# RWKV-7 attention and a GELU MLP on one core: the weights' last conversion step as an integer addition on GpSimd, a scheduler with a refitted picture of the chip, and a search over priorities in the opening

## The chip, the cores and the metric

The kernel runs on one core of a Trainium2 chip. The metric is the device time of one execution in microseconds (us), smaller is better. Before the change the median of three executions is 723.49 us (722.95 to 725.37). The execution that the profiler recorded took 728.5 us, of which 726.7 us lie between its first and last instruction (the span).

## The reference, cut to what matters

For 4 batches, 8 heads, 768 time steps and a head size of 40, a state matrix is carried from step to step; its readings form 3072 tokens of 320 numbers, which go through an MLP with 2048 hidden units:

```python
for t in range(S):
    y[:, :, t] = np.einsum('bhd,bhde->bhe', rt, state)
    Sa = np.einsum('bhde,bhe->bhd', state, at)
    state_decay = state * wt[:, :, None, :] - np.einsum('bhd,bhe->bhde', Sa, bt)
    state = state_decay + np.einsum('bhd,bhe->bhde', vt, kt)
x = y.transpose(0, 2, 1, 3).reshape(B * S, H * D)
h = x @ w_in
g = h * (1.0 / (1.0 + np.exp(-1.702 * h)))
return g @ w_out
```

The inputs are float32, except `w_in` and `w_out`, which come as float64. The kernel receives these as 64-bit words and makes float32 of them on the chip.

## The kernel before, in words

**Tiling.** The 768 steps are cut into 12 chunks of 64 steps. One chunk of two batches is a unit, so there are 24 units, and units 2c and 2c+1 together are chunk c. Inside a unit the recurrence becomes a triangular system. `logarithm` and `decay` make the cumulated decay factors FT, GT and G by running sums (`ps_cum`, `ps_cumc`) and exponentials on ScalarE (ACT). `prep` multiplies them into the inputs (`ak`, `b`, `kh`, `bh`) and makes score matrices (`ps_A`, `ps_RV`). `inverse` inverts the triangular matrix in five levels of doubling (`ps_N`, `ps_level`, `ps_Q`, `ps_T`); each level is a TensorE (PE) product, a copy out of PSUM by ACT or VectorE (DVE), and a DVE transposition. The first four units use a variant of fewer, wider steps (`plain_level`). `solve` puts the state of two units before in (`ps_zT`, `ps_rz`, `ps_B`), solves (`ps_X`, then M, L861), and reads out (`ps_y`, L867 to L900). The result x (L907) goes to DRAM and comes back transposed as `xT` (L917, L921), once for each unit. Only then can `mlp(c)` start: 160 `up` products for a chunk (`ps_up`), the GELU on ACT (`g`, L942), and for each half of a chunk 64 `down` products (`ps_down`), then an addition and a store (L966 to L968). In float32 each product of the program shows as two matmul and two weight-load instructions in the trace.

**The weights.** `weight` (L406 to L447) brings in eight pieces of 128x1280 weights, four of `w_in` (0 to 3), four of `w_out` (4 to 7). Each is 1280 KB of float64 in HBM. The raw words land in one of a few places (`extra`, parts of `w_sb`, or the not yet used part of `xT_all`). The steps are: `rebased` on ACT (L422) scales the high word, read as a float32; `bounded` on DVE (L426) clamps it; `exponent`, two DVE instructions (L430, L431), shifts it left by 3 and keeps sign and exponent apart; `fraction` on DVE (L434) multiplies the low word by 2^-52 and by that power of two; `joined` on DVE (L438) adds both as float32. Pieces 5, 6 and 7 are loaded into a place that an earlier piece must have left first.

**What sets the order.** There is no order in the program text. Every step is a task with a rank, the engines that could do it with a cost in ns for each, what it reads and writes, and a PSUM buffer pair. `Plan.order` is a list scheduler: it runs a picture of the chip forward and gives each free engine the able task of the lowest rank. The picture has a cost for DMA transfers (LATENCY, RATE, SPREAD), the blocks of 256 instructions that PE must fetch (BLOCK, FETCH, and BESIDE for a fetch beside a DMA transfer)[...]. `paced` repeats that four times to spread the MLP products evenly. The tasks are then issued in the order found; each engine, and SP's DMA queue, works through its list strictly in order. ACT needs one table for Ln and Exp and another for GELU. Before, the exponentials of units 4 on are preceded by a load of the table at L542, whether it is the active one or not, and their cost in the picture has 1300 ns for it.

Of the kernel before, what the change touches and what calls it, by code (L numbers as in the profile page):

```python
# [50 lines left out]
class Task:  # L51
    def __init__(self, rank, engines, fn, pair, most, size):
        self.instr, self.sbuf = engines.pop("instr", 0), engines.pop("sbuf", False)
        self.rank, self.fn, self.pair, self.most, self.size = rank, fn, pair, most, size
        self.engines = engines
        self.after, self.then, self.release = set(), [], 0.0


class Plan:
# [5 lines left out]
    BLOCK, FETCH, BESIDE, AHEAD = 256, 3550.0, 0.4, 300.0  # L65
    DELAY = {"PE": 300.0, "DVE": 60.0, "ACT": 60.0, "POOL": 150.0, "SP": 800.0}

    BEGIN = {"PE": 0.0, "ACT": 3300.0, "DVE": 4100.0, "POOL": 9500.0, "SP": 800.0}
    LATENCY, RATE, SPREAD = 1200.0, 400.0, 1.3
# [5 lines left out]
    def add(self, rank, engines, fn, reads=(), uses=(), writes=(), room=(), pair=None, most=None, size=0):  # L75

        t = Task(rank, engines, fn, pair, most, size)
        for key in uses:  # L80
            self.used.setdefault(key, []).append(t)
        for key in reads:
            t.after.update(self.made[key])
            self.used.setdefault(key, []).append(t)
        for name, n in (*writes, *room):
            if name in self.slots:
                old = (name, n - self.slots[name])
                t.after.update(self.made.get(old, ()), self.used.get(old, ()))
        for key in writes:
            self.made.setdefault(key, []).append(t)  # L90
        if pair is not None:
            writers = self.of_pair.setdefault(pair, [])
            t.after.update(o for o in writers if "PE" in o.engines)
            writers.append(t)
        t.after.discard(t)
        self.tasks.append(t)

    def order(self):
# [11 lines left out]
        running, last = [], {}  # L110

        def fits(t):
            if t.pair is None or t.pair in held:
                return True
            clear = sum(p <= now for p in pairs)
            if t.most is None:

                return clear > len({o.pair[0] for o in able if o.most is not None and o.pair not in held and not any(k[0] == o.pair[0] for k in many)})
            return clear > 0 and sum(k[0] == t.pair[0] for k in many) < t.most
# [3 lines left out]
        def fetch(at):  # L123
            took = self.FETCH
            for _ in range(3):
                beside = sum(max(0.0, min(y, at + took) - max(x, at)) for x, y in running[-8:])
                took = self.FETCH + self.BESIDE / self.SPREAD * beside
            return took
# [4 lines left out]

        def fetched(t, start):

            at, left, ns, block = start, t.instr, t.engines["PE"] / t.instr, begun
# [8 lines left out]
        def ahead(t):  # L145

            return (issued % self.BLOCK + t.instr) * fetch(begun) / self.BLOCK - (now + t.engines["PE"] - begun)

        while coming or able:
# [4 lines left out]
            for e in free:  # L154
                if free[e] <= now:
                    took = next((t for t in able if e in t.engines and fits(t) and unread(t, e) <= now), None)
# [5 lines left out]
            if not took:  # L162
                later = [x for x in (*free.values(), *pairs, *(unread(t, e) for t in able for e in t.engines)) if now < x < float("inf")]
                now = min(later + ([coming[0][0]] if coming else []))
                continue
# [3 lines left out]
            end = now + t.engines[e]  # L169
            if e == "PE":  # L170
                end, begun = fetched(t, now)
                issued += t.instr
# [5 lines left out]
            if e == "SP":  # L178
                wire = max(wire, end + self.LATENCY)
                running.append((wire, wire + self.SPREAD * t.size / self.RATE))  # L180
# [21 lines left out]
        assert len(out) == len(self.tasks)  # L202
# [20 lines left out]


@with_exitstack
def rwkv7_gelu_quick(ctx: ExitStack, tc: tile.TileContext, time_d, v_d, w_d, wc_d, ak_d, b_d, rv_d, w_in, w_out, out):
# [16 lines left out]
    ROUNDS, WINDOW, SHARE = 4, 5000.0, 1.0  # L243
    RANKS = [14, 16, 20, 24, 35, 37, 39, 41]
# [74 lines left out]
    padded(nc.vector, rv_t[0])  # L319

# [18 lines left out]
    starts = single("starts", [128, 8, 33])  # L339
    nc.gpsimd.memset(starts, 1.0)  # L340
    nc.gpsimd.memset(starts[:, :, 0], 0.0)
# [15 lines left out]
    for t in ak_t[1], b_t[1], rv_t[1]:  # L357
        padded(nc.gpsimd, t)
# [47 lines left out]
    def weight(n, rank, src):  # L406
# [21 lines left out]
        def exponent(t):  # L428

            nc.vector.tensor_scalar(word(INT32, 1), scale(), 3, -2 ** 23, ALU.logical_shift_left, ALU.bitwise_and)  # L430
            nc.vector.tensor_single_scalar(scale(), scale(), 3, op=ALU.logical_shift_left)  # L431

        def fraction(t):
            nc.vector.scalar_tensor_tensor(word(FP32, 1), in0=word(UINT32, 0), scalar=2.0 ** -52, in1=word(FP32, 1),  # L434
                                           op0=ALU.mult, op1=ALU.mult)

        def joined(t):
            nc.vector.tensor_add(scale().bitcast(FP32), scale().bitcast(FP32), word(FP32, 1))  # L438

        one, two = 170.0 + 0.48 * PIECE, 150.0 + 1.05 * PIECE  # L440
# [4 lines left out]
        plan.add(rank, {"DVE": 2 * one, "sbuf": True}, exponent, reads=T("bounded"), writes=T("exponent"))  # L445
        plan.add(rank, {"DVE": two, "sbuf": True}, fraction, reads=T("exponent"), writes=T("fraction"))
        plan.add(rank, {"DVE": two, "sbuf": True}, joined, reads=T("fraction"), writes=T("weight"))  # L447
# [18 lines left out]

    def load(i):
        for name, of, src, n in (("ak", ak_of, ak_d, 1024), ("time", time_of, time_d, 2 * DM), ("b", b_of, b_d, 512),
                                 ("rv", rv_of, rv_d, 1024), ("RV", RV_of, v_d, 320)):
            rows = [slice(p.start, p.start + D) for p in HALF] if name in ("ak", "b", "rv") else [slice(0, 128)]  # L470

            def go(t, name=name, of=of, src=src, rows=rows):
                for p in rows:
# [3 lines left out]
                     size=sum(p.stop - p.start for p in rows) * n * 4)  # L477
# [10 lines left out]

    def logarithm(i):
        def go(t):  # L490
            if i >= BY_PE:
                nc.scalar.activation(wc_of(i), wc_of(i), ACT.Ln)
            nc.scalar.activation(logw_of(i), logw_of(i), ACT.Ln)
        plan.add(10 * i - 30, {"ACT": (1080.0 if i >= BY_PE else 450.0) + (1300.0 if i >= EARLY + 2 else 0.0)}, go,
# [10 lines left out]
    def decay(i):  # L505
# [19 lines left out]
        def exp_of_product(t):  # L525
            sums = psum(t, "")[:, :, :260].rearrange("p b (j t) -> p b j t", t=65)
# [13 lines left out]
        def exp_channel(t):  # L540
            if i >= EARLY:
                nc.scalar.preload_act_table_set("natural_log_exp_and_others")  # L542
# [8 lines left out]
        if i < BY_PE:  # L551
            plan.add(R, {"ACT": 2400.0}, exp_of_product, reads=T("cum"), writes=T("FT", "GT", "wch"), pair=("cumc", i))
        else:
            plan.add(R, {"ACT": 1600.0 + (1300.0 if i >= EARLY else 0.0)}, exp_channel, reads=T("cum", "sums"), uses=T("wc"),
                     writes=T("FT", "GT", "wch"))
        plan.add(R, {"ACT": 460.0}, lambda t: nc.scalar.activation(G_of(i), psum(t, "")[:, :, :160], ACT.Exp, scale=-1.0),
# [69 lines left out]
    def inverse(i):  # L626
# [36 lines left out]
        def turned(rank, source, reads, n, dst, writes):  # L663
# [10 lines left out]
            plan.add(rank, {"POOL": 1390.0, "DVE": 700.0, "ACT": 1000.0, "sbuf": True}, spread, reads=[key("ES", n, 6)], writes=writes)  # L674
# [254 lines left out]
    def mlp(c):  # L929
# [11 lines left out]
        def gelu(q):  # L941
            plan.add(-45, act(1024), lambda t: nc.scalar.activation(  # L942
# [61 lines left out]
    tasks = plan.paced(list(paces.values()), ROUNDS, WINDOW, SHARE)  # L1004
# [83 lines left out]
```

## Time and profile before

| what | value |
|---|---|
| median of three executions | 723.49 us |
| the profiled execution / its span | 728.5 us / 726.7 us |
| mean granted PE clock | 0.978 |
| PE busy | 677.6 us (93%) |
| DVE / ACT / POOL busy | 430.0 / 356.8 / 187.9 us |
| PE busy, 0 to 150 us | 113.1 us |
| PE busy, 150 to 600 us | 443.0 us |
| first `ps_up` / first `ps_down` matmul starts at | 78.4 / 99.7 us |
| last matmul starts at | 721.5 us |

A page has the busy time of each engine, the span in 40 slices (busy share in tenths; PEclk is the clock that TensorE was granted, in tenths of full speed), and groups of instructions by line, engine, operation and tiles (out<-in), with count, busy time, mean duration, and what ended the idle time before them. The chain of waits is followed back from the last instruction to what released it. The table by stretches gives each engine's busy time in a stretch of the span, then the granted clock and the share of time in which the DMA engines were busy. "issue" stands for a wait that no semaphore explains.

### The profile page before, as it was taken

How to read it: one execution, taken by the hardware profiler on the slowest of the kernel's cores; microseconds unless marked ns; L12 is line 12 of the kernel's file. 1: busy time of each engine (PE TensorE's matmuls, PEld its weight loads, DVE VectorE, ACT ScalarE, POOL GpSimd, SP SyncE). 2: the span in 40 equal slices, each digit the busy share in tenths (PEclk: the TensorE clock that was granted, in tenths of full speed). 3: DMA queues.
4: the chain of work that ended last, by engine and by line, in shares of the span. 5: the costliest groups of instructions: out<-in, count | busy, mean ns of one | idle time of the engine just before them, and what ended most of it. 6: DMA issues, size and time to landing. Idle time of an engine off the chain costs nothing.

```text
span 726.7 us, 43527 instructions
## 1 busy us (share of the span) xinstructions
PE 677.6 (93%) x20256; PEld 572.5 (79%) x20256; DVE 430.0 (59%) x739; ACT 356.8 (49%) x705; POOL 187.9 (26%) x260
## 2 busy tenths in 40 slices
PE   4566997999999999999999999999999989999997
PEld 4555885799788789888888878887889978897564
DVE  6578888956667666666756655755666556431000
ACT  4455655557554554545465455457446446342120
POOL 8104143432431331330350320431530310200000
PEclk9879998999999999999999999999999999999999
DMA  7963542332251341351450440441340230110000
GB/s 216 351 251 93 165 124 86 107 96 78 91 145 55 109 120 49 88 158 32 119 136 22 116 130 31 119 118 39 120 112 23 85 95 5 40 49 30 18 5 20
DMA packets 31861, 69.82 MB, mean 96 GB/s; under 512 B 5056, under 2 KB 14272, under 8 KB 30656
## 3 DMA queue, kind: packets, MB, share of 16 engines
q1 hardware_dynamic: 31680, 67.03, 30.5%
q8 instruction: 159, 2.61, 1.4%
q14 instruction: 22, 0.18, 0.1%
HBM read 59.15 MB, written 7.86 MB: 92 GB/s over the span
## 4 chain that ended last, share of the span: by engine, by line
PE 83%; DVE 5%; issue 3%; ACT 3%; DMA 3%; POOL 2%; SPq 1%; POOLq 0%; DVEq 0%; ACTq 0%
PE ps_down L275 28%; PE ps_up L275 26%; PE ps_level L275 8%; PE ps_y L275 5%; PE ps_B L275 4%; PE ps_X L275 2%; DMA ak<-in_ak 2%; PE ps_Q L275 2%; PE ps_N L275 1%; PE ps_T L275 1%; PE ps_rz L275 1%; PE ps_A L275 1%; PE ps_RV L275 1%; PE ps_zT L275 1%; PE ps_cum L275 1%
## 5 line engine op out<-in xcount | busy, mean ns | idle before, releaser
L275 PE MATMUL ps_up<-xT_all,w_sb 64*64 64x256 f32 x3840 | 249.1, 378 | 2.6 <-ACT g L942 1.5
L275 PE MATMUL ps_down<-w_sb,g 64*64 64x320 f32 x3072 | 244.4, 434 | 3.1 <-DVE w_sb L438 2.5
L275 PEld LDWEIGHTS ps_up<-xT_all,w_sb 64*64 64x64 f32 x3840 | 160.6, 133 | 26.7 <-ACT g L942 1.8
L275 PEld LDWEIGHTS ps_down<-w_sb,g 64*64 64x64 f32 x3072 | 136.2, 134 | 45.3 <-issue 3.1
L670 ACT ACTIVATE EX<-ES,quads 128x256 f32<-128x256 f32 x116 | 52.6, 501 | 49.7 <-DVE ES L665 49.3
L591 POOL TENSOR_TENSOR kh<-time,G 128x320 f32<-128x320 f32 x24 | 22.0, 918 | 185.3 <-PE ps_y L275 91.4
L942 ACT ACTIVATE g<-ps_up 128x1024 f32<-128x1024 f32 x48 | 49.1, 1023 | 40.4 <-PE ps_up L275 40.1
L275 PEld LDWEIGHTS ps_level<-W,EX 64*64 64x64 f32 x2560 | 57.3, 134 | 7.4 <-ACT EX L670 1.4
L716 DVE TENSOR_TENSOR E<-two,ps_level 128x256 f32<-128x256 f32 x80 | 33.2, 415 | 40.3 <-ACT W L714 39.8
L275 PE MATMUL ps_level<-W,EX 64*64 64x64 f32 (+1 forms) x2560 | 55.7, 218 | 0.7 <-ACT EX L670 0.3
L714 ACT COPY W<-ps_level 128x512 f32<-128x512 f32 x51 | 29.8, 585 | 44.0 <-PE ps_level L275 43.9
L275 PE MATMUL ps_level<-PT,EX 64*64 64x64 f32 (+2 forms) x1280 | 36.6, 251 | 11.4 <-DVE EX L686 7.2
L968 DVE TENSOR_TENSOR ob<-ob,ps_down 128x320 f32<-128x320 f32 x24 | 11.6, 484 | 59.4 <-ACT ob L966 59.1
L275 PEld LDWEIGHTS ps_level<-PT,EX 64*64 64x64 f32 x1280 | 34.3, 152 | 15.2 <-DVE EX L686 7.0
L907 POOL TENSOR_TENSOR x<-zr,FT 128x128 f32<-128x128 f32 x84 | 42.8, 539 | 10.4 <-ACT zr L899 10.2
L583 POOL TENSOR_TENSOR ak<-ak,FT 128x512 f32<-128x512 f32 x21 | 27.3, 1299 | 53.2 <-DMA ak<-in_ak 26.2
L845 ACT COPY B<-ps_B 128x416 f32<-128x416 f32 x36 | 18.2, 506 | 44.1 <-PE ps_B L275 43.6
L275 PE MATMUL ps_y<-RV,kh 64*64 64x104 f32 x768 | 36.4, 252 | 2.3 <-DVE M L861 2.2
L665 DVE STREAM_TRANSPOSE ES<-E 128x256 f32<-128x256 f32 x80 | 35.6, 445 | 3.9
L275 PE MATMUL ps_y<-M,bh 64*64 64x104 f32 x768 | 36.5, 252 | 1.3 <-issue 1.3
L275 PEld LDWEIGHTS ps_y<-RV,kh 64*64 64x64 f32 x768 | 30.1, 134 | 6.4 <-DVE M L861 2.4
L861 DVE TENSOR_TENSOR M<-ps_X,later 128x832 f32<-128x832 f32 x24 | 24.5, 1021 | 17.6 <-PE ps_X L275 17.6
(140 smaller groups left out, 1132.9 us busy)
## 6 DMA issues: line engine op xcount, KB each, us to landing
ak<-in_ak SPq DMA_DIRECT2D x48, 160.0 KB
time<-in_time SPq DMA_DIRECT2D x24, 320.0 KB
rv<-in_rv SPq DMA_DIRECT2D x48, 160.0 KB
xT_all<-x_dram SPq DMA_DIRECT2D x48, 160.0 KB
wc<-in_wc SPq DMA_DIRECT2D x20, 264.0 KB
logw<-in_w SPq DMA_DIRECT2D x24, 160.0 KB
b<-in_b SPq DMA_DIRECT2D x48, 80.0 KB
RV<-in_v SPq DMA_DIRECT2D x24, 160.0 KB
```

The source lines that it names most:

```text
L275: nc.tensor.matmul(o, lhsT, rhs, start=start, stop=True, skip_group_check=True)
L583: plan.add(R, {"DVE": 690.0, "POOL": 1270.0, "sbuf": True}, lambda t: of(t.engine).tensor_mul(ahT(), ahT(), FT_of(i)), reads=T("ak", "FT") ...
L591: plan.add(R + 4, {"POOL": 870.0, "DVE": 490.0, "sbuf": True}, lambda t, n=n, dst=dst: of(t.engine).tensor_mul(dst(i)[:, :, :D], by_head(t ...
L665: plan.add(rank, dve(256), lambda t: nc.vector.transpose(ES(n), source(t)), writes=[key("ES", n, 6)], **reads)
L670: nc.scalar.activation(dst[:, :, h], ES(n), ACT.Copy, scale=quads[:, h, :1])
L714: plan.add(rank, any2(512), lambda t: copy(t.engine)(tiles_of(W(n + 1)), blocks(psum(t, ""), 64)), writes=[key("W", n + 1, 5)], pair=pair)
L716: plan.add(rank, dve(256), lambda t: nc.vector.tensor_sub(tiles_of(E(n + 1)), every(two32, [128, 2, 4, 32]), blocks(psum(t, ""), 64)[:, :, ...
L845: plan.add(R, any2(416), lambda t: copy(t.engine)(dst(), psum(t, "")[:, :, :208]), writes=[("Bv", i)] if x and c > 0 else T("B"), pair=(na ...
L861: plan.add(R + 1, dve(832), lambda t: nc.vector.tensor_tensor(M_of(i).rearrange("p (j b) n -> p b j n", b=2), psum(t, "")[:, :, :416].rear ...
L907: of(t.engine).tensor_mul(x[:, b ^ u, b], both(i)[:, at, :64], FT_of(i)[:, at])
L942: plan.add(-45, act(1024), lambda t: nc.scalar.activation(g_of(c * NQ + q).rearrange("p m r n -> p r m n"), psum(t, "").rearrange("p r (m ...
L968: plan.add(-45, dve(320), lambda t: nc.vector.tensor_add(ob_of(serial), ob_of(serial), psum(t, "")[:, 1, :DM]), reads=[("ob", serial)], wr ...
```

## The change

**Weights.** The last steps of a piece are different. `shifted` (one DVE instruction) shifts the scaled high word left by 3 and keeps everything; `rounded` (one DVE instruction) multiplies the low word by 2^-29 and rounds it to an integer in place; `joined` adds both words as 32-bit integers on GpSimd. The DVE instructions of a piece go from five to three, and POOL gets one of 128x1280.

**The picture.** DMA latency, rate and start times, ACT costs, and the cost of a fetch beside a transfer have new values, transfers over 1 MB with one of their own. Matmuls count double when PE was busy for less than 45% of the last 2.6 us. ACT's active table is followed: Ln, Exp and GELU tasks carry its name, a switch costs 1290 ns, and the table of Ln and Exp is loaded only where the order has a switch to it.

**The search.** After `paced`, `refined` tries 300 times to move the ranks of some tasks that start in the first 140 us of the picture by random amounts, and keeps a move if the picture ends earlier.

**The opening by hand.** The zero fills of `b` and `rv` for the second unit go from POOL to DVE, that of `ak` ahead on POOL, `starts` later. The loads of a unit go ak, b, rv, RV, time instead of ak, time, b, rv, RV, and the first two units' have earliest times (CLEAR).

```diff
-        def exponent(t):
-            nc.vector.tensor_scalar(word(INT32, 1), scale(), 3, -2 ** 23, ALU.logical_shift_left, ALU.bitwise_and)
+        def shifted(t):
             nc.vector.tensor_single_scalar(scale(), scale(), 3, op=ALU.logical_shift_left)
-        def fraction(t):
-            nc.vector.scalar_tensor_tensor(word(FP32, 1), in0=word(UINT32, 0), scalar=2.0 ** -52, in1=word(FP32, 1),
-                                           op0=ALU.mult, op1=ALU.mult)
+        def rounded(t):
+            nc.vector.tensor_single_scalar(word(INT32, 1), word(UINT32, 0), 2.0 ** -29, op=ALU.mult)
         def joined(t):
-            nc.vector.tensor_add(scale().bitcast(FP32), scale().bitcast(FP32), word(FP32, 1))
+            nc.gpsimd.tensor_tensor(out=scale(), in0=scale(), in1=word(INT32, 1), op=ALU.add)
...
-        plan.add(rank, {"DVE": 2 * one, "sbuf": True}, exponent, reads=T("bounded"), writes=T("exponent"))
-        plan.add(rank, {"DVE": two, "sbuf": True}, fraction, reads=T("exponent"), writes=T("fraction"))
-        plan.add(rank, {"DVE": two, "sbuf": True}, joined, reads=T("fraction"), writes=T("weight"))
+        plan.add(rank, {"DVE": one, "sbuf": True}, shifted, reads=T("bounded"), writes=T("parts"))
+        plan.add(rank, {"DVE": one, "sbuf": True}, rounded, reads=T("rebased"), writes=T("parts"))
+        plan.add(rank, {"POOL": add}, joined, reads=T("parts"), writes=T("weight"))
...
-    BLOCK, FETCH, BESIDE, AHEAD = 256, 3550.0, 0.4, 300.0
+    OPENING = 140000.0
+    BLOCK, FETCH, AHEAD = 256, 3528.0, 300.0
+    BESIDE, LARGE, BESIDE_LARGE = 0.35, 1e6, 0.63
+    COLD, WINDOW, SHARE = 2.0, 2600.0, 0.45
+    SWITCH = 1290.0
...
-    LATENCY, RATE, SPREAD = 1200.0, 400.0, 1.3
+    LATENCY, RATE, SPREAD = 2010.0, 417.0, 1.3
...
+            if e == "ACT" and t.table:
+                t.load, table = t.table != table, t.table
+                end += self.SWITCH if t.load else 0.0
...
+    def refined(self, tries, seed):
...
+        groups = {}
+        for t in self.tasks:
+            if abs(t.rank) < 10000 and t.start < self.OPENING:
+                groups.setdefault((t.fn.__code__.co_firstlineno, t.rank), []).append(t)
+        keys, rng, best = list(groups), random.Random(seed), end()
+        for _ in range(tries):
+            some = rng.sample(keys, max(1, int(len(keys) * rng.choice((0.003, 0.01, 0.03, 0.1)))))
+            width = rng.choice((0.6, 2.0, 5.0))
...
+            new = end()
+            if new < best:
+                best = new
+            else:
+                for t, rank in old:
+                    t.rank = rank
...
         def exp_channel(t):
-            if i >= EARLY:
-                nc.scalar.preload_act_table_set("natural_log_exp_and_others")
+            tables(t)
...
-    tasks = plan.paced(list(paces.values()), ROUNDS, WINDOW, SHARE)
+    plan.paced(list(paces.values()), ROUNDS, WINDOW, SHARE)
+    tasks = plan.refined(TRIES, SEED)
```

## The prediction

> **What bounds the kernel now.** I read the slices of the page first, then the table by stretches, the waits of TensorE (PE), and the chain of waits. The slices show two different kernels in one:
>
> ```profile
> PE   4566997999999999999999999999999989999997
> PEclk9879998999999999999999999999999999999999
> DMA  7963542332251341351450440441340230110000
> ```
>
> From the eighth slice on (127 us) PE is busy throughout; nothing that another engine does there can gain much. The opening is where time is lost. The stretches (us of PE, PEld, DVE, ACT, POOL, then clock, DMA share, GB/s):
>
> ```profile
> 0.00:20.00 20.00, 10.13 (x346) 8.82 (x347) 13.44 (x21) 8.42 (x27) 15.35 (x51) 1.00 0.76 234
> 20.00:50.00 30.00, 18.34 (x509) 16.28 (x509) 19.47 (x26) 15.48 (x32) 1.48 (x2) 0.72 0.95 335
> 50.00:78.40 28.40, 19.58 (x769) 18.20 (x768) 24.08 (x29) 14.50 (x33) 9.55 (x11) 0.88 0.29 87
> 78.40:110.00 31.60, 30.97 (x844) 26.98 (x840) 26.53 (x33) 19.60 (x32) 9.49 (x9) 1.00 0.51 158
> 110.00:135.00 25.00, 19.06 (x629) 14.55 (x625) 21.62 (x30) 13.06 (x30) 5.99 (x6) 0.86 0.22 75
> 135.00:727.00 592.00, 579.52 (x17192) 487.63 (x17184) 324.89 (x603) 285.70 (x554) 146.07 (x182) 1.00 0.27 77
> ```
>
> The reader is to see two weak places: up to 78.4 us (the first `ps_up` matmul) PE is half idle and slow, and at 110 to 135 us there is a second hole while DVE is the busiest engine. Who is waited for in the first 130 us (us in total, times, longest):
>
> ```profile
> PE ps_level L275 <- DVE EX L686: 7.2, 5, 2.3
> PE ps_level L275 <- issue: 3.8, 2, 2.8
> PE ps_A L275 <- issue: 3.4, 1, 3.4
> PE ps_down L275 <- DVE w_sb L438: 2.0, 1, 2.0
> ```
>
> "issue" is PE waiting for its own instructions. The trace's instruction queue moves 16 KB packets for PE; they start at 24.04, 31.64, 38.70 and 45.79 us, 7.1 to 7.6 us apart while the DMA engines are 95% busy, but 3.6 to 4.6 us apart from 58.96 to 79.3 us. The hole at 110 us is named by the chain (start, us, what):
>
> ```profile
> 108.92 1.28 ACT L542
> ...
> 113.33 2.33 DVE extra L434
> ...
> 117.50 1.75 DVE w_sb L438
> ...
> 119.30 4.54 PE ps_down L275 x32
> ```
>
> The `down` products wait for the last pieces of weights, which wait for DVE: the hole is conversion work in DVE's queue. The 32 matmuls after it take 4.54 us, against 2.15 for 32 at 99.93 in the same chain.
>
> **A sum for the whole span.** At full pace the chain has 80 `ps_up` in 4.32 us (54.0 ns), 224 `ps_down` in 15.07 (67.3 ns) and 64 `ps_y` in 1.43 (22.3 ns); 32 matmuls of 64 columns or fewer follow each other in 0.46 (14.4 ns), and the 96, 128 and 160 columns lie on the same line. Over all 20,256 that is 647.2 us: 207.4 for up, 206.8 for down, 233.0 for the rest. I call time minus the PE work ahead of a point its loss:
>
> - first `ps_up`: 78.4 - 30.7 = 47.7
> - first `ps_down`: 99.7 - 50.4 = 49.3 (so 1.6 more)
> - `ps_y` of unit 3 (133.45 in the chain): 133.4 - 73.6 = 59.8 (10.5 more)
> - end of the last matmul: 722.0 - 647.2 = 74.8 (15.0 more, evenly over the chunks)
>
> 647.2 + 74.8 + 4.7 (last addition and store) is the span of 726.7; with 1.8 around it 728.5. The median of the runs is 5.0 below that one execution, so I take differences from the sum and apply them to 723.5.
>
> [...] L426 takes 784 ns at best and 1889 at 70.36 us, where POOL's multiplications L583 and L588 run. [...]
>
> **The change part by part.**
>
> *DVE's share of the weights.* Undisturbed durations: 0.80 (L426), 0.83 (L430), 0.83 (L431), 1.50 (L434), 1.46 (L438), so 5.42 us for a piece, 43.4 for eight. After: 0.80 + 0.83 + `rounded`. This reads every second word and writes in place; 0.83 is the price of L430, which writes that way, 1.50 that of L434, which reads that way with a second tensor. I take 0.83: 2.46 for a piece, 19.7 for eight, 23.7 less. The high end costs 5.4 of that. The built order gives DVE other work back (two zero fills, copies of Tc). Counted through with such durations, the work ahead of M of unit 3 (L861) falls from 100.4 to 84.5 us, and that up to the last weight step from 99.4 to 77.3.
>
> *POOL's additions.* The nearest rows:
>
> ```profile
> L583 POOL TENSOR_TENSOR ak<-ak,FT 128x512 f32<-128x512 f32 x21 | 27.3, 1299 | 53.2 <-DMA ak<-in_ak 26.2 <-ACT FT L545 18.5 <-PE ps_level L275 3.9
> L591 POOL TENSOR_TENSOR kh<-time,G 128x320 f32<-128x320 f32 x24 | 22.0, 918 | 185.3 <-PE ps_y L275 91.4 <-issue 72.2 <-ACT EX L670 15.1
> ```
>
> From 918 to 1299 ns for 192 more elements is 1.98 ns each: 1299 + 768 x 1.98 = 2.8 us. [...] Eight are 22.6 us[...]. POOL was busy 20 of the 80 us from 30 to 110, so it fits. Behind the additions are queued: T of unit 0 behind piece 0's, `ak` of unit 2 behind piece 1's, x of unit 0 behind piece 2's, x of unit 1 behind piece 3's; `ps_Q`, then `xT` and the first `ps_up`, wait for them. I take nothing for it, because each piece's last DVE step lies beside the PE and DVE steps that these wait for anyway; without that cover 2.8 us each. For the lock I take 5 us of longer DVE instructions in all (0.6 an addition), low 0, high 12.
>
> *Loads.* In the built SP order pieces 0 to 4 come before `ak`, `b` and `rv` of unit 2, so 11.2 MB instead of 8.4 lie up to `ak` of unit 2: 2.8 MB at 335 GB/s, 8.4 us later, about 43 instead of 35. Its first products now stand behind 468 others instead of 368, at about 50 us, so that hides it; without that, up to 8.
>
> *Order up to the first up.* There 868 products now stand ahead, not 812, with 32.9 us of PE work. A block of 256 instructions is 64 products, so 56 more cost 0.9 block of 3.9 us: 81.9, a loss of 49. Against this, one interval in the series of packets (50.04 to 58.96) is 8.9 us with PE waiting for ACT and DVE; the new picture prices cold PE and fetches beside large transfers, so I take it down to 4.0: first up at 77.0, loss 44.
>
> *The hole.* Before, M of unit 3 ended at 131.2, 30.8 after its DVE work. With the same 30.8 and the lock's 5 it ends at 84.5 + 35.8 = 120.3, and `ps_y` starts 2.2 later as it did before (131.2 to 133.4), at 122.5. Its PE work is 74.0: loss 48.5. I add 1.5 for pieces 6 and 7: they should be ready at about 104 and 110 and are due at about 111 and 114. So 50 instead of 59.8.
>
> *Tables and the rest.* Table loads go from 38 to 34 of 1283 ns, 5 us of ACT, off the path after 135. Loss there stays 15, within 3.
>
> Sum: 44 + 2 + 4 + 15 = 65 instead of 74.8, 9.8 less: span 716.9, execution 718.7, and 723.5 - 9.8 = 713.7 us for the median.
>
> **The rivals.**
>
> - *Supply bound (0.20).* Instruction fetch paces the opening, so reordering gains nothing there (loss 49), and the hole keeps 6: 49 + 2 + 6 + 15 = 72, 720.7 us. For it: 7 us packets and the "issue" waits. Against: five waits on DVE in `ps_level`.
> - *All fits (0.13).* First up at 73 (loss 40), no hole (0.5), 13 later: 55.5, 704.2 us.
> - *GpSimd in the way (0.10), slower.* Three of the four results queued behind additions come 2.8 us late, and these are on the serial path: loss 49 + 8.4 at the first up, then 2 + 4 + 15: 78.4, 727.1 us. It decides from a first `ps_up` after about 86.7 us (32.9 + 53.8). For it: POOL works strictly in order[...]. Against: POOL's long idle stretches (185.3 us before L591).
> - *Moved, not removed (0.07).* The picture's end is earlier, the chip's is not: later chunks lose what the opening gains, 723.5 us.
>
> **How the numbers follow.** My case has 0.50 and gives 713.7. A measurement tells about 0.3%, 2.2 us, from no change. Faster: 0.50 + 0.13 + 0.13 of the first rival = 0.76; same 0.07 of it + 0.05 = 0.12; slower 0.10 + 0.02 = 0.12. The range, 705 to 722, leaves out half of the best case below and most of the two last above.
>
> **What would show it.** Five DVE groups for weights become three with 0.8 us means; a POOL group of 128x1280 at 2.8 us; M of unit 3 near 120; no `ps_down` wait over 1 us on weights; `ps_up` from 75 to 79 us. I am wrong if `ps_up` starts after 82, if the hole stays, or if loss after 135 us grows by more than 3.

## The result and the profile after

The changed kernel takes 713.75 us (median of 4 runs, 707.54 to 715.64) against 723.22 us before (median of 4, 720.94 to 725.37). The ratio is 0.986, with a 95% interval of 0.983 to 0.990: some 10 us less. The profiled execution of the changed kernel took 715.64 us with a span of 713.9, the longest of its four; the one of before took 728.5 with 726.7. So the two profiles lie 12.8 us apart, and some 3 us of that are the choice of executions.

Line numbers in the changed file are higher: the matmuls are L330 (L275 before), the weight steps L482 (bounded), L486 (shifted), L490 (rounded) and L494 (added on GpSimd), the table loads L549 (16 of them, for exponentials) and L1008 (17, for gelu), 1283 ns each.

The slices of the page of after, to be held against those of before:

```profile
PE   4667899999999999999999999999999999999997
PEclk9879999999999999999999999999999999999999
DMA  7955351431441341341432241251341230111000
```

PE stays at nine from the sixth slice on instead of from the eighth, and the span ends 13 us sooner. The same stretches (us of PE, PEld, DVE, ACT, POOL, then clock, DMA share, GB/s):

```profile
20.00:50.00 30.00, 19.67 (x578) 18.07 (x573) 21.02 (x30) 15.62 (x26) 12.20 (x8) 0.73 0.86 316
50.00:78.40 28.40, 20.79 (x837) 18.41 (x832) 23.68 (x30) 17.38 (x43) 17.82 (x17) 0.93 0.56 174
78.40:110.00 31.60, 29.74 (x872) 27.66 (x876) 25.72 (x42) 16.53 (x28) 12.43 (x6) 1.00 0.35 108
110.00:135.00 25.00, 25.00 (x817) 22.91 (x813) 20.89 (x35) 15.74 (x32) 12.16 (x10) 1.00 0.38 111
135.00:714.00 579.00, 568.40 (x16880) 466.56 (x16872) 318.01 (x593) 273.55 (x528) 137.21 (x174) 1.00 0.26 76
```

The second hole is gone: PE is busy for all of the 25 us from 110 to 135, at full clock, where it had 19.06 at 0.86. The first weak place remains almost as it was: 19.7 of 30 us and a clock of 0.73 from 20 to 50. GpSimd went from 1.5 to 12.2 us busy there. Who is waited for in the first 130 us:

```profile
PE ps_level L330 <- issue: 5.5, 3, 2.4
PE ps_N L330 <- DMA ak<-in_ak: 5.2, 1, 5.2
PE ps_X L330 <- DVE T L853: 3.3, 2, 2.9
PE ps_cumc L330 <- issue: 2.1, 1, 2.1
```

The 7.2 us for the spread P (`EX`) are down to 0.9, and there is no wait of `ps_down` for weights; "issue" now leads. (The 5.2 us for `ak` lie at the very start, up to 10.6 us; there the kernel before waits 3.9 us for `rv`.)

What "issue" stands for can be read from the 16 KB packets of instructions. In each of the two profiles, 159 of them come for 20,256 matmuls and as many weight loads: 255 of these a packet, near the 256 that the prediction counts for a block. In both profiles each such wait of more than 0.8 us in the first 135 us ends 1.2 to 1.6 us after one of these packets has landed: before, PE goes on at 22.89 us after a packet that landed at 21.38, and at 29.94 after 28.60; after the change at 23.13 after 21.84, and at 29.80 after 28.52. So I read these as waits for instructions. The packet times that the prediction gives stand 11.2 us too late on the clock of the span: its first four packets start at 12.83, 20.43, 27.50 and 34.59 us, and its interval of 8.9 us runs from 38.84 to 47.76.

The chain of waits at the place of the old hole (start, us, what):

```profile
117.65 1.01 PE ps_down L330 x13
118.66 0.68 PE ps_X L330 x30
...
121.61 1.11 PE ps_down L330 x14
122.71 1.39 PE ps_y L330 x62
```

It is matmuls alone, in the lines left out too: DVE is no longer on it. The groups of the weight steps:

```profile
L486 DVE TENSOR_SCALAR w_sb<-w_sb 128x1280 int32<-128x1280 int32 x8 | 11.9, 1487 | 0.1
L482 DVE TENSOR_SCALAR w_sb<-w_sb 128x1280 f32<-128x1280 f32 x8 | 6.5, 814 | 1.5 <-ACT w_sb L478 1.5
L490 DVE TENSOR_SCALAR extra<-extra 128x1280 int32<-128x1280 uint32 x5 | 4.4, 880 | 0.0
L490 DVE TENSOR_SCALAR w_sb<-w_sb 128x1280 int32<-128x1280 uint32 x2 | 1.6, 818 | 0.0
L490 DVE TENSOR_SCALAR xT_all<-xT_all 128x1280 int32<-128x1280 uint32 x1 | 0.8, 785 | 0.0
```

DVE spends 25.2 us on weights, against 48.5 in the profile of before (the sum over its five lines): 23.3 less. On GpSimd:

```profile
L494 POOL TENSOR_TENSOR w_sb<-w_sb,extra 128x1280 int32<-128x1280 int32 x5 | 15.3, 3059 | 7.2 <-DVE extra L490 7.2
L494 POOL TENSOR_TENSOR w_sb<-w_sb 128x1280 int32<-128x1280 int32 x2 | 6.4, 3211 | 3.7 <-DMA time<-in_time 2.0 <-DVE w_sb L490 1.7
L494 POOL TENSOR_TENSOR w_sb<-w_sb,xT_all 128x1280 int32<-128x1280 int32 x1 | 3.5, 3469 | 7.7 <-DVE xT_all L490 7.7
```

### The profile page after: what moved, and what is told of

Read it like the earlier page. It is cut to its first block, busy times and chain, and to the rows that moved or that the text cites. A ratio compares the mean times of both kernels' runs of the same rounds, so it can differ in the third digit from the quotient of the medians.

```text
span 713.9 us, 43522 instructions
## 1 busy us (share of the span) xinstructions
PE 673.0 (94%) x20256; PEld 562.4 (79%) x20256; DVE 423.8 (59%) x747; ACT 347.7 (49%) x683; POOL 204.6 (29%) x260
## 4 chain that ended last, share of the span: by engine, by line
PE 88%; DVE 5%; issue 3%; DMA 2%; ACT 1%; SPq 0%; ACTq 0%; DVEq 0%
PE ps_down L330 29%; PE ps_up L330 28%; PE ps_level L330 9%; PE ps_y L330 4%; PE ps_B L330 4%; PE ps_X L330 2%; PE ps_T L330 1%; PE ps_Q L330 1%; PE ps_rz L330 1%; PE ps_A L330 1%; PE ps_RV L330 1%; PE ps_N L330 1%; PE ps_zT L330 1%; PE ps_cum L330 1%; DMA rv<-in_rv 1%
## 5 line engine op out<-in xcount | busy, mean ns | idle before, releaser
L330 PE MATMUL ps_up<-xT_all,w_sb 64*64 64x256 f32 x3840 | 251.7, 378 | 1.8 <-issue 1.7
L330 PE MATMUL ps_down<-w_sb,g 64*64 64x320 f32 x3072 | 243.0, 431 | 0.8 <-issue 0.6
L330 PEld LDWEIGHTS ps_up<-xT_all,w_sb 64*64 64x64 f32 x3840 | 157.5, 133 | 27.1 <-issue 2.7
L330 PEld LDWEIGHTS ps_down<-w_sb,g 64*64 64x64 f32 x3072 | 131.1, 133 | 45.4 <-issue 2.4
L736 ACT ACTIVATE EX<-ES,quads 128x256 f32<-128x256 f32 x124 | 56.2, 501 | 56.8 <-DVE ES L731 56.4
L1008 ACT ACTIVATE g<-ps_up 128x1024 f32<-128x1024 f32 x48 | 49.1, 1024 | 39.6 <-PE ps_up L330 39.4
L330 PEld LDWEIGHTS ps_level<-W,EX 64*64 64x64 f32 x2560 | 57.5, 134 | 8.3 <-ACT zT L878 1.0
L780 ACT COPY W<-ps_level 128x512 f32<-128x512 f32 x55 | 32.2, 586 | 55.3 <-PE ps_level L330 54.7
L330 PE MATMUL ps_level<-W,EX 64*64 64x64 f32 (+1 forms) x2560 | 55.7, 218 | 0.9 <-ACT zT L878 0.6
L726 POOL TENSOR_TENSOR PT<-two,PT 128x256 f32<-128x256 f32 x18 | 13.1, 728 | 109.8 <-DVE PT L719 105.1
L330 PE MATMUL ps_level<-PT,EX 64*64 64x64 f32 (+2 forms) x1280 | 37.5, 250 | 5.0 <-issue 4.0
L330 PEld LDWEIGHTS ps_level<-PT,EX 64*64 64x64 f32 x1280 | 35.4, 152 | 7.9 <-issue 4.9
L973 POOL TENSOR_TENSOR x<-zr,FT 128x128 f32<-128x128 f32 x80 | 40.9, 539 | 0.0
L330 PE MATMUL ps_y<-RV,kh 64*64 64x104 f32 x768 | 35.7, 251 | 1.4 <-DVE M L927 1.4
L330 PE MATMUL ps_y<-M,bh 64*64 64x104 f32 x768 | 35.6, 249 | 1.2 <-issue 1.2
L649 POOL TENSOR_TENSOR ak<-ak,FT 128x512 f32<-128x512 f32 x16 | 21.5, 1345 | 50.0 <-DMA ak<-in_ak 31.0
L1032 ACT COPY ob<-ps_down 128x320 f32<-128x320 f32 x22 | 9.4, 425 | 53.1 <-PE ps_down L330 53.0
```

Of the source, the lines that this page charges most:

```text
L330: nc.tensor.matmul(o, lhsT, rhs, start=start, stop=True, skip_group_check=True)
L649: plan.add(R, {"DVE": 690.0, "POOL": 1270.0, "sbuf": True}, lambda t: of(t.engine).tensor_mul(ahT(), ahT(), FT_of(i)), reads=T("ak", "FT") ...
L726: plan.add(R, {"DVE": 430.0, "POOL": 750.0, "sbuf": True}, lambda t: of(t.engine).tensor_sub(at(W0_t, i)[:, :, :32], two32.unsqueeze(1).to ...
L736: nc.scalar.activation(dst[:, :, h], ES(n), ACT.Copy, scale=quads[:, h, :1])
L780: plan.add(rank, any2(512), lambda t: copy(t.engine)(tiles_of(W(n + 1)), blocks(psum(t, ""), 64)), writes=[key("W", n + 1, 5)], pair=pair)
L973: of(t.engine).tensor_mul(x[:, b ^ u, b], both(i)[:, at, :64], FT_of(i)[:, at])
```

## The experiments

Each kernel ran in five rounds beside the kernel before, on the same chip. Loss is, as in the prediction, the time at which a matmul starts in the trace minus the PE work ahead of it at full pace; "late" is the loss from `ps_y` of unit 3 to the last matmul. "Same order" means that every engine's instructions follow each other as in the changed kernel, but for the edit. A difference in us between two kernels is the difference of the ratios times 723.2; its uncertainty (+-) joins both 95% intervals, as the root of the sum of squares. Losses are from one profile each.

| kernel | ratio to before | interval | loss, first `ps_up` | loss, `ps_y` of unit 3 | late |
|---|---|---|---|---|---|
| before | 1 | | 47.8 | 59.7 | 15.0 |
| changed | 0.986 | 0.983-0.990 | 46.5 | 48.5 | 13.4 |
| e1 old weight steps, planned again | 1.002 | 0.999-1.004 | 48.5 | 55.0 | 20.6 |
| e2 before + new weight steps | 1.009 | 1.007-1.012 | 46.1 | 52.6 | 25.8 |
| e3 no search | 0.993 | 0.990-0.995 | 46.5 | 50.8 | 18.4 |
| e4 old picture | 0.990 | 0.987-0.992 | 43.7 | 49.1 | 13.5 |
| e5 old weight steps, same order | 0.996 | 0.994-0.998 | 49.6 | 55.6 | 16.8 |
| e6 two additions, same order | 1.005 | 1.003-1.007 | 53.3 | 60.1 | 12.7 |
| e7 no additions, same order | 0.989 | 0.985-0.993 | 47.4 | 49.9 | 14.8 |
| e8 other seed | 0.987 | 0.983-0.992 | 49.2 | 49.8 | 12.9 |
| e9 e2 + tables planned | 0.994 | 0.992-0.997 | 44.1 | 51.8 | 14.7 |
| e10 15 more table loads, same order | 0.988 | 0.984-0.992 | 45.1 | 49.0 | 18.1 |
| e11 35 more table loads, same order | 1.005 | 1.002-1.007 | 44.8 | 47.4 | 24.8 |
| e12 more transfers, same order | 0.996 | 0.993-0.998 | 48.7 | 52.4 | 17.5 |

e10 and e11 leave everything before 135 us as it is in the changed kernel, so with it they are three profiles of one opening: 46.5, 45.1, 44.8 at the first `ps_up` (45.5 in the mean), and 48.5, 49.0, 47.4 at `ps_y` of unit 3. One profile of an opening is good to about 2 us, no better. For the late part it is no better either: e5, e6, e7 and e12 leave it as it is in the changed kernel, and yet the five profiles have 13.4, 16.8, 12.7, 14.8 and 17.5.

### Which part brings it: e1 to e4, e8

The edits, e2's being that of e1 turned round, in the kernel before:

```diff
 e1
-        plan.add(rank, {"DVE": one, "sbuf": True}, shifted, ...)
-        plan.add(rank, {"DVE": one, "sbuf": True}, rounded, ...)
-        plan.add(rank, {"POOL": add}, joined, ...)
+        plan.add(rank, {"DVE": 2 * one, "sbuf": True}, exponent, ...)
+        plan.add(rank, {"DVE": two, "sbuf": True}, fraction, ...)
+        plan.add(rank, {"DVE": two, "sbuf": True}, joined, ...)
 e3
-    TRIES, SEED = 300, 1
+    TRIES, SEED = 0, 1
 e4
-    BLOCK, FETCH, AHEAD = 256, 3528.0, 300.0
-    BESIDE, LARGE, BESIDE_LARGE = 0.35, 1e6, 0.63
-    COLD, WINDOW, SHARE = 2.0, 2600.0, 0.45
-    BEGIN = {... "DVE": 5500.0, "POOL": 10000.0, ...}
-    LATENCY, RATE, SPREAD = 2010.0, 417.0, 1.3
+    BLOCK, FETCH, AHEAD = 256, 3550.0, 300.0
+    BESIDE, LARGE, BESIDE_LARGE = 0.4 / 1.3, 1e6, 0.4 / 1.3
+    COLD, WINDOW, SHARE = 1.0, 2600.0, 0.45
+    BEGIN = {... "DVE": 4100.0, "POOL": 9500.0, ...}
+    LATENCY, RATE, SPREAD = 1200.0, 400.0, 1.3
 e8
-    TRIES, SEED = 300, 1
+    TRIES, SEED = 300, 3
```

> The changed kernel with the weight steps of before (two DVE instructions for the exponent, the fraction and the sum on DVE, with their old costs for the planner); picture, tables and search stay new, so the order is planned again. Theory A (mine): the gain comes from about 24 us of conversion work that left DVE's queue. Then most of it is gone here: 719 to 723 us, and ps_y of unit 3 starts at 129 us or later. Rival B: picture and search brought the gain: 713 to 716 us, ps_y of unit 3 before 124 us. Rival C: any new plan moves the time by several us whatever it contains: no relation to the parts.

> The kernel before with the new weight steps alone (shift, rounding on DVE, integer addition on GpSimd, with their new costs); old picture, no search, old order of loads. A: 714 to 718 us, ps_y of unit 3 at 122 to 126 us. B: 719 to 723 us. C: anything, also slower than before.

> The changed kernel with 0 tries of the search, all else as changed. A: 713 to 717 us, the search worth at most 2 us of it. B: 718 us or more, since the search made the order of the opening. C: no relation.

> The changed kernel with the picture's constants of before (fetch 3550, 0.4 / 1.3 beside any transfer, no cold PE, old begins of DVE and POOL, latency 1200, rate 400); weights, search, tables and order of loads stay new. A: 713 to 717 us. B: 718 us or more, because a search over a wrong picture finds nothing that the chip repeats.

> The changed kernel with another seed of the search (3 instead of 1), all else the same. A: 711 to 717 us, within 3 us of the changed kernel, since the search only rearranges what the lighter DVE queue leaves. C: over 4 us away in either direction; then parts of the change measured by a new plan are told apart only down to that size.

Measured. Planned anew without the new weight steps, nothing is left of the gain: e1 stands at 1.002, 11 us (+-3) behind the changed kernel. Its new picture and search do shorten the opening, from 59.7 to 55.0, and it gives 5.6 back in the late part. B, with its 713 to 716 us, is out. But e1 doesn't price the weight steps: 7.2 us of what it loses against the changed kernel are lost late, by the profiles, after the last weights are converted, and with as many table loads (34 in all). The cause of that is open. And the weight steps alone don't bring the gain either: e2 is 6.8 us slower than before, where A wanted 714 to 718 us. This was the miss of the study. By `ps_y` of unit 3 e2 is ahead of before by 7.1 us (125.6 us, as A had it), and then it loses 25.8 instead of 15.0. Why is taken up with e9 to e11.

The hole at 110 us doesn't tell the parts apart. It closes with a new plan and the old steps (e1, the first line) and with the new steps under the old planner (e2, the second), where the kernel before had PE busy for 19.06 us:

```profile
110.00:135.00 25.00, 24.00 (x728) 18.80 (x724) 20.57 (x29) 12.84 (x23) 6.28 (x8) 1.00 0.35 117
110.00:135.00 25.00, 24.20 (x805) 20.72 (x799) 21.19 (x44) 11.52 (x23) 9.58 (x7) 1.00 0.27 77
```

The loss up to `ps_y` of unit 3 does: a closed hole can mean that the loss came earlier.

With the new steps in place, the search is worth 4.6 us (+-3.2; e3), an interval that A's 2 lies in. Where it brings that isn't shown: the profiles differ by 2.3 us in the opening and 5.0 late, little more than profiles of one order differ by. The picture's constants, the double count of matmuls among them, are settings of the planner and aren't told from nothing (2.4 +-3.2; e4). Another seed gives the same time within its interval, which speaks against C for the search: two searches over the same parts end 0.9 us apart (+-4.0). For a plan made from other parts C isn't excluded, as the late part of e1 shows. The opening by hand (zero fills, order and earliest times of the loads) had no run of its own.

### The arithmetic with the order held: e5

Each piece's three DVE slots, taken in the order in which they come, do what the kernel before did, and its sum on DVE stands in the slot of the addition (`bounded` and `rounded` call `next_step` as `shifted` does):

```diff
+        steps = []
+        def next_step():
+            steps.append(n)
+            if len(steps) == 1:
+                nc.vector.tensor_scalar(scale().bitcast(FP32), scale().bitcast(FP32), least, most, ALU.max, ALU.min)
+            elif len(steps) == 2:
+                nc.vector.tensor_scalar(word(INT32, 1), scale(), 3, -2 ** 23, ALU.logical_shift_left, ALU.bitwise_and)
+                nc.vector.tensor_single_scalar(scale(), scale(), 3, op=ALU.logical_shift_left)
+            else:
+                nc.vector.scalar_tensor_tensor(word(FP32, 1), in0=word(UINT32, 0), scalar=2.0 ** -52, in1=word(FP32, 1),
+                                               op0=ALU.mult, op1=ALU.mult)
...
         def shifted(t):
-            nc.vector.tensor_single_scalar(scale(), scale(), 3, op=ALU.logical_shift_left)
+            next_step()
...
         def joined(t):
-            nc.gpsimd.tensor_tensor(out=scale(), in0=scale(), in1=word(INT32, 1), op=ALU.add)
+            nc.vector.tensor_add(scale().bitcast(FP32), scale().bitcast(FP32), word(FP32, 1))
```

> The order of the changed kernel kept instruction for instruction, but the three DVE steps of a piece and the addition do what the kernel before did: bounded, two instructions for the exponent, the fraction, and the sum on DVE in the place of the addition on GpSimd; nothing on GpSimd for weights. This puts about 24 us of DVE work back without moving anything. A: first ps_up 1 to 4 us later and the hole at 110 to 135 us back, 720 to 727 us. B: the order carries the gain: 713 to 717 us. C doesn't speak here, the order being the same.

Measured: ratio 0.996. So the new order with the old steps, tables included, is worth 2.9 us (1.3 to 4.4), and the new steps in that order 7.1 us (+-3.0): about seven tenths of the gain. It is an order that was searched for the lighter steps; e1 and e2 show that the two parts don't simply add. The size is A's; the place is not. The stretches of e5, in the same columns:

```profile
20.00:50.00 30.00, 15.23 (x488) 13.95 (x492) 24.33 (x32) 14.77 (x25) 6.35 (x6) 0.74 0.87 318
110.00:135.00 25.00, 24.35 (x755) 21.74 (x751) 20.61 (x38) 18.18 (x32) 5.70 (x6) 1.00 0.27 70
```

No hole comes back at 110. The loss grows in two places. The first is up to the first `ps_up`, 3.1 us more than in the changed kernel (4.1 more than the mean of its three profiles). In the new order the weights come earlier in DVE's queue: the second piece gets its last step at 45.1 us in e5 and at 57.0 before, and weight steps take 14.8 us of DVE between 20 and 50 us (8.6 before). There PE does 4.4 us less than in the changed kernel, and one `ps_X` at 48.6 us waits 5.6 us for T from DVE (2.9 in the changed kernel).

The second place is from the first `ps_up` (82.3) to the first `ps_down` (103.1): 4.0 us more. PE hardly waits there, but it is slow. Its granted clock is 0.50 from 82 to 86 us and 0.62 from 86 to 90, where the changed kernel has 1.00 from 78 us on (e5 twice, then the changed kernel):

```profile
82.00:86.00 4.00, 3.75 (x36) 2.04 (x35) 3.15 (x7) 2.76 (x8) 1.28 (x1) 0.50 0.32 103
86.00:90.00 4.00, 4.00 (x98) 3.65 (x95) 2.06 (x3) 0.53 (x1) 0.00 (x0) 0.62 0.00 0
82.00:86.00 4.00, 4.00 (x152) 3.85 (x148) 3.42 (x6) 2.34 (x3) 1.87 (x1) 1.00 0.29 86
```

From 82.3 to 89 us half of the pace is 3.4 us, an estimate from these clocks, and most of the 4.0. The low clock follows a sparse stretch: in e5 PE is busy for 1.8 us from 74 to 78. In the changed kernel such a stretch (1.8 us from 70 to 74) comes earlier, the clock is 0.57 from 74 to 78, and full when the `ps_up` products begin. So in e5 the late opening cost twice: 3.1 us as delay, and by this estimate 3.4 more because these products began at a low clock.

### What the additions on GpSimd cost: e6, e7

```diff
 e6
+            nc.gpsimd.tensor_tensor(out=word(INT32, 0), in0=scale(), in1=word(INT32, 1), op=ALU.add)
             nc.gpsimd.tensor_tensor(out=scale(), in0=scale(), in1=word(INT32, 1), op=ALU.add)
 e7
-            nc.gpsimd.tensor_tensor(out=scale(), in0=scale(), in1=word(INT32, 1), op=ALU.add)
```

By the lock, the prediction and the next two expectations mean that a DVE instruction takes longer beside work on GpSimd. In the profile of before, L426 started at 70.36 us during a multiplication on GpSimd (L588, 70.05 to 71.57), took 1.89 us instead of 0.78, and ended 0.68 us after it.

> The order of the changed kernel kept, each addition on GpSimd made twice (the first into the low words of the raw piece, which are dead by then). 8 x 2.96 = 23.7 us more on GpSimd in the first 110 us. If GpSimd has room and the lock costs little: within 1 us of the changed kernel. A: the lock and the products queued behind the additions cost part of their length, the longer first stage (7 us of stretched DVE instructions) coming once more: 2 to 5 us more than the changed kernel. If GpSimd is the bound of the opening: 8 us more or above.

> The order of the changed kernel kept, the eight additions on GpSimd left out, so that the fraction of the weights is not added; nothing takes their place. This prices what the additions still cost. GpSimd has room: within 1 us of the changed kernel. A: 1 to 3 us less, first ps_up at 77 to 78 us, DVE instructions of the bounding and shifting no longer over 1 us beside them. Lock as the main rest of the loss: 5 us less or more.

Measured: leaving them out gains nothing (2.1 us slower, +-3.9, so a gain above 1.8 us is excluded); making them twice costs 13.4 us (+-3.0), which was the outermost of the three cases of e6. One addition a piece fits, two don't. The chain of waits of e6 shows where it breaks:

```profile
67.58 0.90 DVE extra L490
...
68.55 2.96 POOL extra L494
...
71.59 0.20 POOL w_sb L495
71.79 3.04 issue
74.82 2.51 POOL x L974 x4
...
77.68 5.32 DMA x_dram<-x
...
83.57 3.24 DMA xT_all<-x_dram
...
86.86 1.18 PE ps_up L330 x17
```

The chain puts 3.04 us of the second addition down to "issue"; the two together last 6.3. x of unit 1, the second half of chunk 0, stands behind them on GpSimd, then goes out to memory and back (8.6 us), and the first `ps_up` waits for that: 86.0 us against 79.2. This is the rival "GpSimd in the way" of the prediction, at the place and near the time (86.7) that it named. In the changed kernel the cover holds.

In e7 the DVE instructions are shorter, as the group shows against 1487 ns in the changed kernel:

```profile
L486 DVE TENSOR_SCALAR w_sb<-w_sb 128x1280 int32<-128x1280 int32 x8 | 8.1, 1017 | 0.1
```

Yet PE gains nothing from it. In the changed kernel T and then the `ps_X` at 46.70 us come right behind the longest of the eight, and `ps_X` waits 2.9 us; in e7, without that long instruction, it still waits 2.5 (at 45.86). What holds PE there instead was not found. PE's waits for instructions in the first 130 us are 13.6 us in e7, but 10.6, 13.0 and 10.3 in the three profiles of the changed kernel's opening, so they don't set e7 apart.

### Late in the kernel: table loads, e9 to e11

The trace of e2 has 59 table loads on ACT, where before has 38 and the changed kernel 34:

```profile
L942 ACT ACT_TABLE_LOAD x24 | 30.8, 1283 | 0.4
L542 ACT ACT_TABLE_LOAD x20 | 25.7, 1283 | 0.4
L556 ACT ACT_TABLE_LOAD x7 | 9.0, 1283 | 0.1
L492 ACT ACT_TABLE_LOAD x7 | 9.0, 1283 | 0.1
L308 ACT ACT_TABLE_LOAD x1 | 1.3, 1283 | 0.8 <-PEq L1081 0.8
```

The old planner doesn't know which table is loaded. Lighter weight steps moved its order so that gelu and the exponentials alternate more often.

```diff
 e9: e2, and in order() with the `tables` helper and the table costs of the changed kernel
+            if e == "ACT" and t.table:
+                t.load, table = t.table != table, t.table
+                end += 1290.0 if t.load else 0.0
 e10, in the exponential over time
+            if t.start > 135000.0:
+                nc.scalar.preload_act_table_set("natural_log_exp_and_others")
+            else:
+                tables(t)
 e11, in tables(t), which the logarithms and exponentials call
-        if t.load:
+        if t.load or t.start > 135000.0:
```

> The kernel before with the new weight steps and with the planner's knowledge of ScalarE's table (a load only where the last task used another table, and its cost charged there); old picture, no search, old order of loads. The weight steps alone gave a loss of 56 us up to about 195 us (60.6 before) but 78.4 at the end (74.7 before), with 59 table loads instead of 38. Theory D: the later loss came from these loads, which the old planner doesn't see. Then with 34 loads the part after 195 us loses 11 to 15 us, and the time is 715 to 720 us. Rival E: the order of the later stages was bad for another reason, and only the search or the new picture mends it: 725 us or more.

> The order of the changed kernel kept, with 15 table loads of 1283 ns added after 135 us (one ahead of each exponential over time, 19 us of ScalarE). D: ScalarE is late for gelu and the exponentials at times, as in the run with the weight steps alone, which lost 8 us with 25 loads more than the changed kernel: 3 to 6 us more than the changed kernel, all of it after 135 us. E: ScalarE has room (270 us busy of 579), within 1 us.

> The order of the changed kernel kept, with a table load ahead of every logarithm and exponential after 135 us: 35 loads of 1283 ns more than the changed kernel, 45 us of ScalarE. With 15 more the profile showed 4 us more loss after 195 us, but the times left 0 to 5 us open. D: the loads cost TensorE some 0.25 to 0.4 us each, so 8 to 14 us more than the changed kernel, ratio to the kernel before 0.997 to 1.006. E: ScalarE has room for them, as it is busy less than half of the time after 135 us: at most 3 us more, ratio 0.990 or below; then the late loss of the run with the weight steps alone was its order and not its loads.

Measured: e9 stands at 0.994 where e2 stood at 1.009, 11.0 us (+-2.7) less, and its late part is 14.7 instead of 25.8, with 34 loads. But e9 is also planned anew. e10 left the price open (1.2 +-4.1 us for 15 loads; 4.7 us of loss late in its profile). e11, in the changed kernel's order, settles the price: 35 loads cost 13.5 us (+-3.2), and the late loss rises from 13.4 to 24.8, well above the 12.7 to 17.5 of one order.

```profile
L549 ACT ACT_TABLE_LOAD x51 | 65.4, 1283 | 0.9
L1008 ACT ACT_TABLE_LOAD x17 | 21.8, 1283 | 0.3
```

That is 0.33 (profile) to 0.39 us (times, +-0.09) for a load that takes ACT 1.28 us, although ACT is busy for only about half of that stretch (47% in the changed kernel, 55% in e11). The 25 loads that e2 has more than e9 are worth 8 to 10 us at this price, of the 11.0 measured. Theory D is kept; that it was the loads that slowed e2 itself is a match in size with another order, not shown by an edit in e2's own.

### What still holds the first stage: e12

```diff
             nc.sync.dma_start(raw(), src)
+            spare = dram.tile([128, PIECE // 2], INT64, tag=f"spare{n}", name="spare_dram")
+            nc.sync.dma_start(spare, src[:, :PIECE // 2])
```

> The order of the changed kernel kept, but with each of the eight pieces of weights half a piece is also copied from memory to a spare place in memory, on the same queue right behind it: 0.65 MB eight times, about 2 us of the DMA engines each, five of them before the loads of unit 2. It tests what holds the first stage, where taking the additions away gained nothing. If transfers and instruction supply hold it: first ps_up 6 to 10 us later, 5 to 9 us more than the changed kernel. If the transfers have slack, as I took it for the 8.4 us by which the loads of unit 2 move: first ps_up within 2 us, at most 2 us more in the end.

Measured: 6.7 us (+-3.1) more than the changed kernel, in the range of the first theory, but not in its place: the first `ps_up` is only 2.3 us later (81.5; 3.3 later than the mean of the three profiles), the first `ps_down` 6.0 (102.0 instead of 96.0). The stretches of e12:

```profile
20.00:50.00 30.00, 19.00 (x564) 17.53 (x568) 21.80 (x30) 15.29 (x25) 10.93 (x7) 0.73 0.95 371
50.00:78.40 28.40, 21.08 (x817) 19.20 (x815) 22.68 (x28) 16.55 (x41) 16.32 (x17) 0.86 0.73 245
82.00:86.00 4.00, 4.00 (x51) 2.56 (x53) 1.16 (x2) 1.23 (x4) 0.00 (x0) 0.50 0.14 51
```

The last line is why `ps_down` is later still: as in e5, PE is busy at a low clock after the first `ps_up`, 0.50 from 82 to 86 us, up to about 88 us.

The DMA engines' share rises from 0.86 to 0.95 and from 0.56 to 0.73. Transfers have little slack, but they are not the only bound up to the first `ps_up`; how the rest divides between them, the supply of instructions and the serial steps of each unit was not taken apart.

None of the twelve beats the changed kernel by more than the intervals.

## Why the prediction was right, point by point

The number (713.7) and the sign hold. Of the terms 44, 2, 4 and 15, the profile has 46.5, 0.1, 1.9 and 13.4: none is off by more than 2.5 us, about what one profile can tell. In their own order:

- *DVE's share of the weights: right.* 23.3 us less were measured, 23.7 forecast. The expected 0.8 us means hold for L482 and nearly for L490, not for L486 (1487 ns).
- *GpSimd's additions: priced a little low.* 3.06 to 3.47 us in the mean by the operands' places instead of 2.8: 25.2 in sum instead of 22.6. "I take nothing for it" was right (e7), and so was the mechanism that would have made it wrong (e6). The margin is under one more addition a piece.
- *DVE beside the additions: longer, and of no account.* The 5 us taken for it were an estimate of mine, worked out from no trace. One L486 that starts at 42.81 beside an addition (42.12 to 45.57) takes 3.45 us: it ends 0.69 after the addition, about its own undisturbed length. Another starts at 85.77 beside an addition that ends at 87.60, and ends 0.69 after it too. The eight L486 carry 5.6 us over their undisturbed 0.79; 1.8 of it stay when there are no additions (e7), so 3.8 are theirs, where 5 were charged. Charging it to M of unit 3 was close for the time (M ended at 121.1, forecast 120.3), but e7 shows that without the additions `ps_y` isn't earlier.
- *Order up to the first `ps_up`: the step that failed, by 1 to 2 us.* I took one interval of 8.9 us between packets down to 4.0, for a loss of 44. It came out at 46.5, 45.1 and 44.8 in three profiles, first `ps_up` at 79.2, 77.9 and 77.5 instead of 77.0. I also read the interval at the wrong place, 11.2 us late. At its own place, 38.84 to 47.76 us, PE waits 2.3 us for `EX` from DVE and its clock is 0.56 (38 to 48 us), and I had named nothing that shortens these. In the changed kernel the interval from 37.37 to 44.70 is still 7.3 us: a wait of 1.9 for T from GpSimd ends in it, and one of 2.9 for T from DVE begins. In the other two profiles the longest intervals are 7.4 and 6.9. The packets ahead of it come a little faster, 6.1 to 6.8 us apart from 14.06 to 33.56 us instead of 7.1 to 7.6, but the waits for instructions up to 130 us are no shorter: 10.3 to 13.0 us against 9.5.
- *Up to the first `ps_down`: mis-sized.* 2 forecast, 0.1 measured (46.6), because there is no wait for weights left at all, which also settles pieces 6 and 7.
- *The hole: right in time, for a reason only half right.* `ps_y` of unit 3 at 122.7 in the chain against 122.5, loss 48.5 as worked out; the 1.5 added for pieces 6 and 7 weren't needed. But the hole closes with either part alone (e1 and e5, e2), so its closing doesn't show that lighter steps were needed for it. What they bring in the new order is the loss up to this point, 7.1 us (e5), and there the heavy steps would have cost before 90 us and not at 110.
- *Loads: true for the wait, unpriced otherwise.* No wait for `ak` of unit 2 appears. But added transfers cost in e12, so it isn't shown that 2.8 MB moved forward were free.
- *Tables: costed at nothing, which was the wrong step.* "5 us of ACT, off the path after 135" is 4 loads at 0.33 to 0.39 us, 1.3 to 1.6 us. The late part fell from 15.0 to 13.4. That the loads are what moved it is a match in size, not shown: one order alone gives 12.7 to 17.5, and the late parts of other plans with 28 to 38 loads lie between 12.9 and 20.6.

Sum: 44 + 2 + 4 + 15 = 65 was forecast and 61.9 measured in one execution, which would be 710.6; the runs' median lies 3 us above this. The first term was measured 2.5 above its forecast and the others 5.6 below theirs together, and the profiled executions stand at different distances from their medians (5.0 us above before, 1.9 after). That 713.7 met 713.75 so closely is luck; that some 10 us are gained is not. The rival "supply bound" had its first half right (reordering gains little before the first `ps_up`) and its second wrong (the hole went). "Moved, not removed" fits two halves of the change by their profiles, and not the whole: e1, whose late part is slower without a cause found, and e2 with its table loads.

## What to carry to other kernels

The worth of a lighter step depends on the order around it: here the same arithmetic gave +6.8 us in a plan that didn't see the table loads, -4.2 with them seen, and -10 with picture, search and opening by hand. Before calling an engine's time "off the path" because it is half idle, price one instruction more of that kind by adding some in a held order. A hole that closes is no proof of its cause; compare the loss up to a point behind it. And when an engine is eased, ask what is late next: here PE's waits for instructions stayed (10.3 to 13.0 us up to 130 us, 9.5 before), and in e5 a late opening was paid for again at a clock of 0.50 to 0.62.

## What the runs showed of the hardware

- An integer addition of 128x1280 on GpSimd takes 2.94 us at best and up to 3.48; with both operands in `w_sb` it took 2.98 and 3.45.
- A DVE instruction of 0.79 us that started during such an addition ended 0.69 us after it, two times in the changed kernel. Leaving all eight additions out gained nothing (2.1 us slower, +-3.9).
- A 1.28 us table load on ACT cost the whole kernel 0.33 to 0.39 us (35 more of them, e11), with ACT busy 47% of the time after 135 us without them and 55% with them.
- PE's "issue" waits of over 0.8 us in the first 135 us, before and after the change, ended 1.2 to 1.6 us after a 16 KB packet of instructions had landed; 159 packets came for 20,256 matmuls and as many weight loads.
- PE's granted clock was about half for some 10 us in e5 and e12 (79 to 89 and 78 to 88 us; 0.50 in both from 82 to 86), after 4 us in which PE was busy for 1.8 and 1.6 us; most of it passed with PE busy.
- 5.2 MB more copied within memory during the opening, eight times 0.65 MB, cost 6.7 us (+-3.1; e12).
